# A planner with a new count of instruction blocks and new weights, chunk 3 in a pair, and all decays on VectorE

## The chip, the cores and the metric

The kernel runs on one core of a Trainium2 chip, in float32. Its engines are TensorE (PE, matrix products; PEld is its weight load), VectorE (DVE), ScalarE (ACT), GpSimd (POOL) and SyncE (SP, which here issues DMA transfers). The metric is the device time of one execution in microseconds (us), the median over several runs. The kernel before takes 751.02 us (five runs, 746.96 to 753.35).

## The reference, cut to what matters

A linear attention with a decaying state is computed step by step over 768 tokens, for 4 batches and 8 heads of width 40. Its output goes through a two-layer network with SiLU (320 to 2048 to 320) for all 3072 tokens.

```python
# r, k, v, w, a, b: (4, 8, 768, 40); state: (4, 8, 40, 40)
for t in range(S):
    y[:, :, t] = np.einsum('bhd,bhde->bhe', rt, state)
    Sa = np.einsum('bhde,bhe->bhd', state, at)
    state_decay = state * wt[:, :, None, :] - np.einsum('bhd,bhe->bhde', Sa, bt)
    state = state_decay + np.einsum('bhd,bhe->bhde', vt, kt)
...
x = np.ascontiguousarray(attn_out.transpose(0, 2, 1, 3)).reshape(B * S, H * D)
h = x @ w_in                      # (3072, 320) @ (320, 2048)
g = h * (1.0 / (1.0 + np.exp(-h)))
return (g @ w_out).astype(np.float32)
```

## The kernel before, in words

**Chunks.** The sequence is cut into NN = 12 chunks of 64 tokens. For each chunk the 32 problems (batch and head) are worked at once, and the 256 tokens of the chunk (4 batches of 64) then go through the network. Inside a chunk the step-by-step recurrence is replaced by the inverse of a triangular 64 x 64 matrix for each problem; only the state G passes from chunk to chunk.

**The pieces for chunk n.** `load` and `load_r` read the inputs on SyncE's queue. `prepare` makes running products of the decays with two scans on DVE (L505 and L523, with small helpers L511 to L524 between them), multiplies them onto the inputs (`aside`, L542, writes `kb` for b in two halves and for k in one; `scale`, L532, multiplies `a`), and forms products of tokens with tokens on PE (`between`, L560; `sv`, L621) and transposes (`turn`, L646, copied out by ACT into `kt`). `chain` advances the state: `right` (L987) and its sum into R on DVE (L997), `solve` (L1011), `solve_t` (L1042), the state's transpose (L1072) and `update` (L1099). `read` computes the output: `look` (L1141), `write` (the state's part L1178, the chunk's part L1191) and `scaled` (L1202). `bring` carries it through DRAM into `xt`. `moe` is the network: `full` (L1271), `rest` (L1284), the SiLU `gate` on ACT (L1294), `second` (L1311) and the copy to `ot` (L1323).

**Two ways to the inverse.** Chunks below NS = 4 take `special`: blocks of 16 are inverted on DVE (the multiply L672, the reduction L673 and a copy L696 in `dots` and `steps`), then PE joins them with `both` (L790), `turn` (L803) and three `more` (L835), each followed by an add on DVE (L850). Chunks 4 to 11 are taken two at a time by `inverse(k)`: blocks of 32 of both chunks are inverted on DVE alone, read from `md` in DRAM into `mi` and written back to `zd` and `xd`. Then `merge(n)` brings ZQ and X from there, and joins the blocks with `first` (L915), a copy of ZQ (L283 on ACT, L287 on DVE) and `second` (L944).

**What sets the order.** Nothing is left to the order of the source: every operation is given to the planner `Plan` with its engine, an estimated cost, what it reads and writes, a priority `pri`, the number `k` of its matmuls and the PSUM or SBUF buffers (`Room`) that it needs. `order()` is a list scheduler over all five engines. For each engine it looks at the operations that are ready, and the engine that can start earliest gets one. Among those that can start within SLACK of the earliest it takes the lowest `pri`; when small matmuls have run for more than MOST, it prefers large ones (`k` below 33). `walk` models that PE's instructions are fetched in blocks of 256 and stretches a start where a block would be missing. The list that comes out is written as the program, and each engine runs its own instructions in that order, waiting on semaphores.

**Who computes the decays.** `aside` and `scale` run on DVE for chunks 0 to 3 and on POOL for chunks 4 to 11:

```python
e, cost = ("DVE", 1.25) if n < 4 else ("POOL", 2.6)
add(e, cost + 0.1, partial(aside, e, 1), [vk, bk], ["B"], pri)
add(e, cost, partial(scale, e, A, Z), allw, [("a", i3)], pri)
add(e, cost, partial(aside, e, 0), [vk, kk], ["K"], pri + 0.1)
```

The functions that the change touches:

Of the kernel before, what the change touches and what calls it, by code (L numbers as in the profile page):

```python
# [32 lines left out]
class Plan:  # L33
# [8 lines left out]
    def add(self, engine, cost, do, r=(), w=(), pri=0, rooms=(), k=0, size=0.0, after=0.0):  # L42
        op = dict(
            engine=engine, cost=cost, do=do, pri=pri, rooms=rooms, k=k, size=size, n=len(self.ops), after=after
        )
        before = set()
        for k in r:
            if isinstance(k, tuple) and k[0] == "@":
                before.add(self.wrote[k[1]])
                continue  # L50
            if k in self.wrote:
                before.add(self.wrote[k])
            self.read.setdefault(k, []).append(op["n"])
        for k in w:
            if k in self.wrote:
                before.add(self.wrote[k])
            before.update(self.read.get(k, ()))
            self.wrote[k], self.read[k] = op["n"], []
        before.discard(op["n"])
        op["before"] = before  # L60
        self.ops.append(op)
        return op

    HOP = {"SP": 0.1, "ACT": 0.15, "PE": 0.15, "DVE": 0.15, "POOL": 0.2}
    SLACK = {"SP": 0.0, "ACT": 0.1, "PE": 0.4, "DVE": 0.15, "POOL": 0.1}
    RATE, LAND = 300.0, 2.0
    MOST, SHARE = 1.5, 2.0

    def walk(self, start, cost, k, keep=False):


        fetched, count, t = list(self.fetched), self.count, start
        step = cost / max(k, 1)
        end = count + k
        while True:
            i = len(fetched) - 2
            go, gate = 256 * (i + 1), 256 * (i + 2) - 64
            if count <= go < end:
                t += (go - count) * step
                count = go  # L80
            elif not count > go:
                break
            begin = max(t + 0.4, fetched[-1] + 2.6) if not go < count else max(t, fetched[-1] + 2.6)
            fetched.append(begin + 1.3)
            if gate < end:
                t = max(t + (gate - count) * step, begin + 1.4) if gate > count else max(t, begin + 1.4)
                count = max(count, gate)
        t += (end - count) * step
        if keep:
            self.fetched, self.count = fetched, end  # L90
        return t

    def order(self):
        ops = self.ops
        self.fetched, self.count = [0.0, 0.0], 0
# [7 lines left out]
        mixed, out, held = 0.0, [], {}  # L103
        queue = dict.fromkeys(("SP", "ACT", "POOL"), 0.0)
        for op in ops:
            op["ready"] = op["after"]
        while len(out) < len(ops):
            best = None
            for e, some in ready.items():
                starts = []  # L110
                for op in some:
# [7 lines left out]
                    if e == "PE" and s < 1e8:  # L119
                        lost = self.walk(s, op["cost"], op["k"]) - s - op["cost"]  # L120
# [3 lines left out]
                least = min(x for _, x, _ in starts)  # L124
                near = [x for x in starts if x[1] <= least + self.SLACK[e]]
                if e == "PE" and mixed > self.MOST:
                    near = [x for x in near if x[2]["k"] < 33] or near
                s, _, op = min(near, key=lambda x: (x[2]["pri"], x[2]["n"]))
# [6 lines left out]
            if e == "PE":  # L135
                mixed = mixed + op["cost"] if op["k"] > 32 else max(0.0, mixed - self.SHARE * op["cost"])
            at[e] = end = self.walk(s, op["cost"], op["k"], True) if e == "PE" else s + op["cost"]
# [29 lines left out]
def kernel(  # L167
# [147 lines left out]
    WS, NS, NL, ND, NP = 1024, 4, 0, 1, 3  # L315
# [23 lines left out]
    def weights(n):  # L339
# [42 lines left out]
        for h in range(2):  # L382
            for i in (1, 0):

                def sum_(h=h, i=i):
                    nc.tensor.matmul(
                        pf.tile[:, h],
                        lhsT=ident,
                        rhs=words[:, 512 * h : 512 * h + 512, i].bitcast(F32),
                        start=i == 1,  # L390
                        stop=i == 0,
                    )

                add("PE", 0.97, sum_, me, [(pf, h)], pri, [pf], 2)
# [93 lines left out]
    def prepare(n):  # L488
# [60 lines left out]
        e, cost = ("DVE", 1.25) if n < 4 else ("POOL", 2.6)  # L549
# [19 lines left out]
        add("PE", 1.14, partial(between, 1, pb_), ["B", ("a", i3)], [pb_, ("sb", i2)], pri, [pb_], 128)  # L569
# [17 lines left out]
        else:  # L587
            for b in range(2):
                for c in range(2):
                    q0 = 64 * i2 + 32 * c + 16 * b  # L590
                    r0 = 64 * b + 32 * c
                    dma(
                        lambda q0=q0, r0=r0, c=c: nc.sync.dma_start(
                            md[n // 2 % 2][q0 : q0 + 16].rearrange("q s t -> s q t"),
# [4 lines left out]
                        [("md", n // 2 % 2, i2, b, c)],  # L599
# [3 lines left out]
        add("PE", 1.14, partial(between, 0, pk), ["K", ("a", i3)], [pk], pri + 0.5, [pk, sk], 128)  # L603
# [25 lines left out]
        add("PE", 1.14, sv, [sk, ("v", i2, 0), ("v", i2, 1)], [pv, ("R", i3)], pri + 0.6, [pv, sk], 128)  # L629
# [9 lines left out]
        for b in range(2):  # L639
# [15 lines left out]
            add("PE", 0.75, turn, ["K", "B"], [pt, ("kt", i3, b)], pri + 0.7, [pt], 33)  # L655
# [76 lines left out]
    def special(n):  # L732
# [82 lines left out]
        for part in parts:  # L815
            XI_, X_ = keyed(("XI",), part), keyed(("X2", i2), part)
            k = len(part)
            add("PE", 0.57 * k, partial(both, pm[part], lambda b, g: S_[half(b), g, :], block, part), [("sb", i2), *mik], [pm[part], *XI_], pri, [pm[part]], 64 * k)
            add("PE", 0.3 * k, partial(turn, pd[part], part), mik, [pd[part]], pri, [pd[part]], 16 * k)
# [5 lines left out]
        for k in range(3):  # L825
# [17 lines left out]
            for part in parts:  # L843
                XI_, X_, Y_ = keyed(("XI",), part), keyed(("X2", i2), part), keyed(("tmp",), part)
                l, py = len(part), py_[part]
                add("PE", 0.87 * l, partial(more, part, py), [*XI_, *(Y_ if k else X_)], [py], pri, [py], 64 * l)
# [16 lines left out]
    def inverse(k):  # L863
        i = k % 2
        pri = 10 * (2 * k - 2) + 7
# [15 lines left out]
    def merge(n):  # L881
        pri = 10 * (n - 1) + 5
        i, n2 = n // 2 % 2, n % 2
        X = Xs[n2].rearrange("p (q t) -> p q t", q=Q)
        S_ = sbs[n2].rearrange("p (q t) -> p q t", q=Q)
# [11 lines left out]
        for x in range(2):  # L897
            for c in (1, 0):
# [7 lines left out]
                    [("X", n2, x, c)],  # L906
# [17 lines left out]
        add("PE", 0.8, first, [("sb", n2), ("Zt", 0), ("Zt", 1)], [p1, ("Q", 0), ("Q", 1)], pri, [p1], 128)  # L924
# [28 lines left out]
        add("PE", 1.2, second, [("Q", 0), ("Q", 1), ("X", n2, 0, 1), ("X", n2, 1, 1)], [p2, ("XM", n2, 0), ("XM", n2, 1)], pri, [p2], 128)  # L953
        for x in range(2):
# [8 lines left out]
                [("XM", n2, x)],  # L963
# [4 lines left out]
    def chain(n):  # L968
# [10 lines left out]
        if n:  # L979
# [21 lines left out]
            add("PE", 1.2, right, [("a", i3), "G"], [pa], pri, [pa], 128)  # L1001
            add("DVE", vec(640), total, [pa], [("R", i3)], pri, [pa])
        pw_ = {part: Room("pair", 2) for part in halves(n)}
        if not last:
# [14 lines left out]
            add("PE", 1.14, solve, [*xkeys, ("R", i3)], [pu], pri, [pu], 128)  # L1019
# [39 lines left out]
        for part in halves(n):  # L1059
# [4 lines left out]
            add("PE", 0.57 * l, partial(solve_t, part, pw), [*xp, ("R", i3)], [pw, *[("ut", m) for m in part]], p_, [pw], 64 * l)  # L1064
            add("ACT", act(512 * l), partial(turned, part, pw), [pw], [("ut", m) for m in part], p_, [pw])
        if n:
# [14 lines left out]
            add("PE", 0.75, turn, ["G"], [pt, "GT"], pri + 0.3, [pt], 33)  # L1081
# [11 lines left out]
        if not last:  # L1093
# [13 lines left out]
            add("PE", 1.3, update, [*ktk, *vk, ("u", i2, 0), ("u", i2, 1)], [pg], pri, [pg], 128)  # L1107
# [15 lines left out]
    def read(n):  # L1123
# [8 lines left out]
        for m in range(2):  # L1132
# [16 lines left out]
            add("PE", 1.14, look, rk + vtk + [("ut", m)], [pl], pri, [pl, la], 128)  # L1149
# [15 lines left out]
        py_, yx = {part: Room("pair", 2) for part in parts}, Room("lam", 1)  # L1165
# [6 lines left out]

        def write(part, py):
            if n:
                for o in problems("m", "z", "x", "j", "b"):
                    b, j, x, m, z = (o[k] for k in "bjxmz")
                    hh, c = 8 * j + 4 * m + 2 * z + x, 4 * m + 2 * z + x
                    nc.tensor.matmul(  # L1178
                        py.tile[rows(j), b, c * C : c * C + C],
                        lhsT=GT[rows(b), (8 * j + c) * D : (8 * j + c) * D + D],  # L1180
                        rhs=rs[rows(b), hh, :],
                        start=fresh(py, b, j),
                        stop=False,
                        skip_group_check=True,
                    )
# [23 lines left out]
        for part in parts:  # L1209
            used = [lam[m] for m in part]  # L1210
            cost = 3.05 if n else 0.95 * len(part)
            add("PE", cost, partial(write, part, py_[part]), ktk + rk + used + (["GT"] if n else []), [py_[part]], pri, [py_[part], *used], 256 if n else 64 * len(part))
# [50 lines left out]
    def moe(n):  # L1263
# [4 lines left out]
        def full(g):  # L1268
            for k in range(2):
                for f in range(4):  # L1270
# [4 lines left out]
                        start=g % 2 == 0 and k == 0 and f % 2 == 0,  # L1275
                        stop=g % 2 == 1 and k == 1,
# [3 lines left out]
        def rest(g0):  # L1280
            for g in (g0, g0 + 1):
                for f in (0, 2, 1, 3):
# [5 lines left out]
                        start=g % 2 == 1 and f % 2 == 0,  # L1288
                        stop=g % 2 == 0,
# [9 lines left out]
        for g in (0, 2):  # L1299
            a_, b_ = rooms[g], rooms[g + 1]  # L1300
            w_ = lambda g: [("wi", g)]
            add("PE", 3.6, partial(full, g), [*xk[0], *xk[1], *w_(g)], [a_, ("gts", g), ("gts", g + 1)], pri + g, [a_], 32)
            add("PE", 2.0, partial(rest, g), [*xk[2], *xk[3], ("wi3",)], [a_, b_], pri + g + 0.1, [a_, b_], 32)
            add("PE", 3.6, partial(full, g + 1), [*xk[0], *xk[1], *w_(g + 1)], [b_], pri + g + 0.2, [b_], 32)
# [14 lines left out]
        for b in range(2):  # L1319
            for part in range(4):  # L1320
                need = sorted({("wo", c) for c in range(4 * part * DM // WS, ((4 * part + 4) * DM - 1) // WS + 1)})
                add("PE", 2.17, partial(second, b, part), [("gts", part), ("gts", 3), *need], [po[b]], pri + 4 + b + part * 0.1, [po[b]], 16)
# [23 lines left out]
    for n in range(NN):  # L1346
# [18 lines left out]
        if n + 3 == NS:  # L1365
            eye()
        if n % 2 == 1 and NS < n + 3 < NN + 1:
            inverse(n // 2 + 1)
# [157 lines left out]
```

## Time and profile before

| | before |
|---|---|
| median of five runs | 751.02 us (746.96 to 753.35) |
| profiled execution, its own time | 751.41 us |
| its span | 749.6 us |
| mean granted clock of TensorE | 0.982 |
| PE busy | 683.1 us, 91% |
| DVE busy | 396.0 us, 53% |
| ACT busy | 196.0 us, 26% |
| POOL busy | 81.8 us, 11% |
| longest PE groups | L1311 227.8 us, L1271 178.7 us, L1284 49.0 us |
| decays on POOL | L542 48.4 us in 24 instructions |

The profile is one execution, taken by the hardware profiler. The span is cut into 40 equal slices; a digit is the busy share of an engine in tenths, and `PEclk` is the clock that TensorE was granted, in tenths of full speed. The list of waits says which group of instructions stood idle for whom: total us, number of times, longest. A timeline row gives the start, the time from the first start to the last end, the engine, the source line, what was written and read, the tile, the count, and in brackets the idle time before it with its releaser. A matmul's start to the next one's start is the better measure of its price, since ends are modelled. A matmul in float32 is shown as two instructions, so a call of `second` with four products is eight.

### The profile page before, as it was taken

The numbers are of one execution on the slowest core, as the hardware profiler recorded it, in microseconds if no ns is written. First come the engines' busy times: TensorE is split into PE (matmuls) and PEld (weight loads), VectorE is DVE, ScalarE is ACT, GpSimd is POOL, SyncE is SP. The second block draws the span as 40 slices with busy tenths as digits, with TensorE's granted clock in tenths as the row PEclk, the third lists the DMA queues.
The fourth block names the chain that finished last, engine by engine and source line by source line (L and its number), as shares of the span: only waits on it lengthen the run. The fifth ranks groups of instructions, "written<-read, shape, count | busy, mean of one in ns | idle before, by whom it ended". The sixth has DMA issues, their size and how long they took to land.

```text
span 749.6 us, 27622 instructions
## 1 busy us (share of the span) xinstructions
PE 683.1 (91%) x12810; PEld 540.6 (72%) x12810; DVE 396.0 (53%) x567; ACT 196.0 (26%) x240; POOL 81.8 (11%) x63
## 2 busy tenths in 40 slices
PE   2198898899979998999998999998999999999995
PEld 2176686687768777787777777777777878778773
DVE  6867889574624397245596344496244193320000
ACT  3264355032223113313213113213213203111010
POOL 3200000003004004003220013130013000000000
PEclk9999999999999999899999999999999999999999
DMA  7672833660532434254533344532341403121000
GB/s 245 153 229 74 275 119 94 173 163 17 144 89 87 117 102 88 83 135 126 132 94 73 61 120 130 133 94 66 63 121 44 110 18 84 39 67 40 18 1 22
DMA packets 116956, 75.72 MB, mean 101 GB/s; under 512 B 64546, under 2 KB 113634, under 8 KB 116194
## 3 DMA queue, kind: packets, MB, share of 16 engines
q1 hardware_dynamic: 112328, 63.10, 31.8%
q0 software_dynamic: 2096, 10.49, 4.0%
q8 instruction: 102, 1.67, 0.9%
q10 hardware_dynamic: 2410, 0.30, 0.3%
q14 instruction: 20, 0.16, 0.1%
HBM read 59.64 MB, written 13.83 MB: 98 GB/s over the span
## 4 chain that ended last, share of the span: by engine, by line
PE 62%; DVE 21%; DMA 6%; issue 3%; SPq 3%; ACT 2%; POOL 1%; ACTq 0%; DVEq 0%; POOLq 0%
PE pair L1311 21%; PE pair L1271 14%; DVE XI L672 6%; PE pair L1284 4%; DVE XI L673 4%; DMA wz<-in_wT 3%; PE pair L1141 3%; PE pair L835 3%; PE pair L1191 3%; DVE wz L523 2%; DVE kbv L505 2%; PE pair L560 2%; PE pair L1099 2%; POOL kb L542 1%; PE pair L1178 1%
## 5 line engine op out<-in xcount | busy, mean ns | idle before, releaser
L1311 PE MATMUL pair<-wo,gts 128*128 128x320 f32 x768 | 227.8, 449 | 2.8 <-ACT kt L659 2.8
L1311 PEld LDWEIGHTS pair<-wo,gts 128*128 128x128 f32 x768 | 144.9, 194 | 60.3 <-issue 3.5
L1271 PE MATMUL pair<-xt,wi 128*128 128x256 f32 x768 | 178.7, 387 | 3.9 <-ACT vu L285 1.9
L1271 PEld LDWEIGHTS pair<-xt,wi 128*128 128x128 f32 x768 | 143.8, 192 | 28.6 <-issue 4.0
L1294 ACT ACTIVATE gts<-pair 128x1024 f32<-128x1024 f32 x48 | 49.1, 1023 | 177.5 <-PE pair L1284 88.8
L542 POOL TENSOR_TENSOR kb<-kbv 128x512 f32<-128x512 f32 (+1 forms) x24 | 48.4, 2033 | 324.3 <-DVE wc L512 222.4
L560 PE MATMUL pair<-a,kb 40*64 40x64 f32 x1536 | 30.5, 238 | 28.9 <-DVE a L532 28.9
L560 PEld LDWEIGHTS pair<-a,kb 40*64 40x64 f32 x1536 | 27.8, 151 | 34.1 <-issue 18.4
L1284 PE MATMUL pair<-xt,wi 64*128 64x256 f32 x384 | 49.0, 391 | 3.2 <-DVE ot L1323 2.0
L1323 DVE COPY ot<-pair 128x320 f32<-128x320 f32 x24 | 11.7, 488 | 71.4 <-PE pair L1311 69.7
L673 DVE TENSOR_REDUCE XI<-XI 128x64 f32<-128x512 f32 (+9 forms) x68 | 46.9, 690 | 2.3
L1284 PEld LDWEIGHTS pair<-xt,wi 64*128 64x128 f32 x384 | 35.1, 187 | 12.4 <-issue 5.6
L1153 DVE TENSOR_TENSOR lam<-pair,ml 128x1024 f32<-128x1024 f32 x24 | 29.0, 1220 | 24.1 <-PE pair L1141 24.1
L672 DVE TENSOR_TENSOR XI<-XI,mi 128x1024 f32<-128x1024 f32 (+8 forms) x48 | 36.2, 754 | 5.4 <-DMA mi<-md 4.3
L1202 DVE TENSOR_TENSOR lam<-pair,wz 128x1024 f32<-128x1024 f32 (+1 forms) x13 | 14.8, 1142 | 45.5 <-PE pair L1191 45.3
L523 DVE TENSOR_TENSOR_SCAN wz<-wz,zt 128x1024 f32<-128x1024 f32 x12 | 30.5, 2538 | 0.4
L1141 PEld LDWEIGHTS pair<-r,vut 40*64 40x64 f32 x1536 | 24.8, 135 | 6.1 <-issue 5.3
L606 DVE TENSOR_TENSOR lam<-pair,ml 128x1024 f32<-128x1024 f32 x12 | 14.6, 1220 | 27.2 <-PE pair L560 23.9
L1141 PE MATMUL pair<-r,vut 40*64 40x64 f32 x1536 | 27.7, 221 | 1.1 <-issue 1.0
L505 DVE TENSOR_TENSOR_SCAN kbv<-wz,zt 128x1024 f32<-128x1024 f32 x12 | 27.5, 2292 | 1.0
L1085 ACT COPY GT<-pair 128x640 f32<-128x640 f32 x11 | 7.6, 692 | 74.3 <-PE pair L1072 74.3
L285 ACT ACTIVATE sb<-pair 128x1024 f32<-128x1024 f32 x12 | 12.3, 1022 | 56.3 <-PE pair L560 56.2
(146 smaller groups left out, 728.3 us busy)
## 6 DMA issues: line engine op xcount, KB each, us to landing
wz<-in_wT SPq DMA_DIRECT2D x12, 512.0 KB, 4.2
kbv<-in_bT SPq DMA_DIRECT2D x12, 512.0 KB, 3.6
a<-in_aT SPq DMA_DIRECT2D x12, 512.0 KB, 4.7
kbv<-in_kT SPq DMA_DIRECT2D x12, 512.0 KB, 4.4
r<-in_rT SPq DMA_DIRECT2D x48, 96.0 KB, 2.7
vut<-in_vT SPq DMA_DIRECT2D x48, 96.0 KB, 3.2
vu<-in_v SPq DMA_DIRECT2D x24, 160.0 KB, 4.2
out<-ot SPq DMA_DIRECT2D x48, 80.0 KB, 2.0
```

What stands on the lines that cost most here:

```text
L505: nc.vector.tensor_tensor_scan(back(V), back(W[:, 2 : 2 + Q * C]), zt, 1.0, ALU.mult, ALU.add)
L523: nc.vector.tensor_tensor_scan(Z, Z, zt, 0.0, ALU.mult, ALU.add)
L542: TTn[engine].tensor_tensor(out=at_(kb, place(is_b, first), (576 * step, 4 // step), (128, 4), (1, C)), in0=blocks((kf, bf)[is_b]), in1=bl ...
L560: nc.tensor.matmul(room.tile[half(b), j, g * C : g * C + C], lhsT=kb[rows(j), place(is_b, q) : place(is_b, q) + C], rhs=A[rows(j), q * C : ...
L672: nc.vector.tensor_tensor(out=at_(tmp, 0, *dims), in0=x, in1=y, op=ALU.mult)
L673: nc.vector.tensor_reduce(out=out_, in_=at_(tmp, 0, *dims), axis=AX.X, op=ALU.add)
L1141: nc.tensor.matmul(pl.tile[half(1 - b if role else b), b, c * C : c * C + C], lhsT=vut[rows(b), role, hu, :], rhs=rs[rows(b), hh, :], star ...
L1153: lambda pl=pl, la=la: nc.vector.tensor_tensor(out=la.tile.rearrange("p (q t) -> p q t", q=Q), in0=pl.tile.rearrange("p a b -> p (a b)").r ...
L1271: nc.tensor.matmul(rooms[g].tile[:, f // 2, (f % 2) * T : (f % 2) * T + T], lhsT=wi[:, k, (4 * g + f) * 128 : (4 * g + f) * 128 + 128], rh ...
L1284: nc.tensor.matmul(rooms[g].tile[:, h, (f % 2) * T : (f % 2) * T + T], lhsT=wi3[half(h), g * 256 + (f % 2) * 128 : g * 256 + (f % 2) * 128 ...
L1294: nc.scalar.activation(out=gts[:, 4 * g * T : 4 * g * T + 4 * T], in_=rooms[g].tile.rearrange("p a b -> p (a b)"), func=AF.Silu)
L1311: nc.tensor.matmul(po[b].tile[:, 0, 0:DM], lhsT=g4[:, f, 128 * b : 128 * b + 128], rhs=wo[:, f, :], start=f == 0, stop=f == NF - 1,)
```

## The change

- The planner chooses, on each engine, the operation with the least of (start + time lost + URGE x `pri`) in place of the window SLACK; the limit MOST and SHARE is gone.
- Each PE operation gets a `shape` (F, R, T, Q, H, S); going from one shape to another costs LEAVE of the old and ENTER of the new in the plan.
- `walk` is written anew: blocks are counted as `count // 256`, with a gate at 194 instructions of a block, and a step costs double before 42 us.
- The estimated costs and counts of most PE operations are changed; the estimates don't alter the operations themselves.
- NS goes from 4 to 3: chunks 0 to 2 take `special`; the pairs are (3, 4), (5, 6), (7, 8), (9, 10), and 11 alone. There are five `inverse` and nine `merge` instead of four and eight.
- `aside` and `scale` of every chunk run on DVE.
- `write` is split into two planned operations, `write_state` and `write`.
- `moe` issues full, full, rest for each pair of groups instead of full, rest, full; `second` waits for the last `full` through a key `ff` instead of through the gate buffer.

```diff
-    SLACK = {"SP": 0.0, "ACT": 0.1, "PE": 0.4, "DVE": 0.15, "POOL": 0.1}
     RATE, LAND = 300.0, 2.0
-    MOST, SHARE = 1.5, 2.0
+    COLD = 42.0
+    URGE = {"SP": 0.0, "ACT": 0.03, "PE": 0.05, "DVE": 0.1, "POOL": 0.02}
+    LEAVE = {"F": 0.09, "R": 0.2, "T": 0.13, "Q": 0.13, "H": 0.12, "S": 0.11}
+    ENTER = {"F": 0.08, "R": 0.1, "T": 0.03, "Q": 0.03, "H": 0.03, "S": 0.03}
+
+    def turn(self, op):
+
+        a, b = self.shape, op["shape"]
+        if a == b or {a, b} == {"R", "T"}:
+            return 0.03 if a != "F" else 0.0
+        return self.LEAVE[a] + self.ENTER[b]
...
-        fetched, count, t = list(self.fetched), self.count, start
-        step = cost / max(k, 1)
-        end = count + k
-        while True:
-            i = len(fetched) - 2
-            go, gate = 256 * (i + 1), 256 * (i + 2) - 64
...
+        fetched, count, t = self.fetched[-2:], self.count, start
+        step, end = cost / max(k, 1) * (2 if start < self.COLD else 1), count + k
+        have = len(self.fetched)
+        while count < end:
+            block = count // 256
+            gate = 256 * block + 194
+            if have == block + 1:
+                fetched.append(max(t + 0.4, fetched[-1] + 2.6) + 1.3)
+                have += 1
+            if count >= gate:
+                t = max(t, fetched[-1] + 0.1)
+            to = min(end, gate if count < gate else 256 * block + 256)
+            t += (to - count) * step
+            count = to
...
-                        lost = self.walk(s, op["cost"], op["k"]) - s - op["cost"]
+                        lost = self.walk(s + self.turn(op), op["cost"], op["k"]) - s - op["cost"]
...
-                least = min(x for _, x, _ in starts)
-                near = [x for x in starts if x[1] <= least + self.SLACK[e]]
-                if e == "PE" and mixed > self.MOST:
-                    near = [x for x in near if x[2]["k"] < 33] or near
-                s, _, op = min(near, key=lambda x: (x[2]["pri"], x[2]["n"]))
+                urge = self.URGE[e]
+                s, _, op = min(starts, key=lambda x: (x[1] + urge * x[2]["pri"], x[2]["n"]))
...
-    WS, NS, NL, ND, NP = 1024, 4, 0, 1, 3
+    WS, NS, NL, ND, NP = 1024, 3, 0, 1, 3
...
-        e, cost = ("DVE", 1.25) if n < 4 else ("POOL", 2.6)
+        e, cost = "DVE", 1.25
...
-            cost = 3.05 if n else 0.95 * len(part)
-            add("PE", cost, partial(write, part, py_[part]), ktk + rk + used + (["GT"] if n else []), [py_[part]], pri, [py_[part], *used], 256 if n else 64 * len(part))
+            if n:
+                add("PE", 0.9, partial(write_state, py_[part]), [*rk, "GT"], [py_[part]], pri, [py_[part]], 128)
+            add("PE", 0.87 * len(part), partial(write, part, py_[part]), ktk + used, [py_[part]], pri, [py_[part], *used], 64 * len(part), shape="H")
...
-            add("PE", 3.6, partial(full, g), [*xk[0], *xk[1], *w_(g)], [a_, ("gts", g), ("gts", g + 1)], pri + g, [a_], 32)
-            add("PE", 2.0, partial(rest, g), [*xk[2], *xk[3], ("wi3",)], [a_, b_], pri + g + 0.1, [a_, b_], 32)
-            add("PE", 3.6, partial(full, g + 1), [*xk[0], *xk[1], *w_(g + 1)], [b_], pri + g + 0.2, [b_], 32)
+            for i, x in enumerate((a_, b_)):
+                add("PE", 3.45, partial(full, g + i), [*xk[0], *xk[1], *w_(g + i)], [x, ("ff", n), ("gts", g + i)], pri + g + 0.1 * i, [x], 32, shape="F")
+            add("PE", 1.72, partial(rest, g), [*xk[2], *xk[3], ("wi3",)], [a_, b_], pri + g + 0.2, [a_, b_], 32, shape="R")
...
-        if n + 3 == NS:
-            eye()
-        if n % 2 == 1 and NS < n + 3 < NN + 1:
-            inverse(n // 2 + 1)
+            if n + 3 == NS:
+                eye()
+        if n + 1 >= NS and (n + 1 - NS) % 2 == 0 and n + 1 < NN:
+            inverse((n + 1 - NS) // 2)
```

## The prediction, made before the changed kernel ran

> **What bounds the kernel now.** I read the page first (busy shares, slices, chain), then the waits of TensorE, then the timeline around those waits, and last the granted clock in windows of 3.4 us.
>
> ```profile
> span 749.6 us, 27622 instructions
> PE 683.1 (91%) x12810; PEld 540.6 (72%) x12810; DVE 396.0 (53%) x567; ACT 196.0 (26%) x240; POOL 81.8 (11%) x63
> PE   2198898899979998999998999998999999999995
> DVE  6867889574624397245596344496244193320000
> PEclk9999999999999999899999999999999999999999
> ```
>
> TensorE (PE) is busy for 683 of 749.6 us and close to full in every slice after the third. So what counts is PE's own work, the price of its order, and its few idle places. VectorE (DVE) has 47% free over the whole, but little in slices 5 to 7 (75 to 131 us).
>
> ```profile
> PE pair L560 <- DVE a L532: 28.9, 2, 15.4
> PE pair L790 <- DMA mi<-zs: 3.2, 2, 2.2
> PE pair L835 <- DVE XI L850: 2.7, 2, 2.0
> PE pair L915 <- DMA ZQ<-zd: 2.7, 2, 1.4
> PE pair L646 <- POOL kb L542: 1.9, 1, 1.9
> ```
>
> Columns: total, times, longest. The first row is the start (13.5 and 15.4 us, over at 42 us): it waits for the first chunks' loads and scans, which the change leaves as they are, so it is priced at nothing. All other PE waits together are under 30 us; a new order can win those, what switching between kinds of matmul costs, and the instructions it no longer issues.
>
> ```profile
> 252.28 2.42 PE L1311 MATMUL pair<-wo,gts 128*128 128x320 f32 x8
> 254.63 1.11 PE L1178 MATMUL pair<-r,GT 40*40 40x64 f32 x64
> ...
> 371.72 15.34 PE L1311 MATMUL pair<-wo,gts 128*128 128x320 f32 x56
> 387.00 1.14 PE L987 MATMUL pair<-G,a 40*64 40x40 f32 x64
> ```
>
> Columns: start, time, engine and line. From start to next start, eight L1311 matmuls alone between small ones take 254.63 - 252.28 = 2.35 us; in the long run, (387.00 - 371.72) / 7 = 2.18. So the large side of one interruption is at least 0.17 us, and 0.198 against the 2.153 of the calls inside other runs. On the small side a half of L560 takes 1.09 us between two large ones and 0.93 among small ones: 0.16.
>
> **The change, part by part.** The profiled execution took 751.4 us beside its span of 749.6; the median shown is 751.0, so the sum is made on 751.4 and may stand for the median.
>
> (1) Chunk 3 leaves the special path. PE loses `both` (64 matmuls, 1.09 us), `turn` (0.64) and three `more` (2.01 each): 7.8 us. It gains a `merge` (L915 0.77, L944 1.13): 1.9. Net -5.9. The waits inside that path go too:
>
> ```profile
> 210.73 1.98 PE L790 MATMUL pair<-mi,sb 64*64 64x64 f32 x62 [2.17 <-DMA mi<-zs]
> ...
> 224.37 2.08 PE L835 MATMUL pair<-XI 64*64 64x64 f32 x64 [2.03 <-DVE XI L850]
> ...
> 230.76 2.08 PE L835 MATMUL pair<-XI 64*64 64x64 f32 x64 [0.66 <-DVE XI L850]
> ```
>
> 2.17 + 2.03 + 0.66 = 4.9. After the first, the clock fell:
>
> ```profile
> 206.90:210.30 3.40, 1.65 (x68) 1.12 (x66) 0.49 (x1) 0.69 (x1) 0.00 (x0) 1.00 0.51 113
> 210.30:213.70 3.40, 2.97 (x82) 2.88 (x84) 0.00 (x0) 0.95 (x1) 0.00 (x0) 0.50 0.52 135
> ```
>
> Columns: window, length, busy time of PE, PEld, DVE, ACT, POOL, granted clock. 3.4 us at half clock lose 1.7. Together -5.9 - 4.9 - 1.7 = **-12.5**. Bounds: -14 if the order closes up better, -7.6 if as many us of waits come back around the new merge. There are now five of the 32-step inverses instead of four, and nine merges for eight. The fifth inverse is 31 us of DVE and DMA steps (the four took 31.1, 35.8, 34.9 and 29.5 from the first load to the copy out) in place of the 16-step one of chunk 3; PE's other work hides it, as it hides the four. Without that cover it would be the wait of rival A. On SyncE's queue chunk 3 loses 18 transfers (8 `ms`, `xs`, `zs`, 8 `mi`) and gains 14 (4 `md`, `mi`, 2 `zd`, `xd`, 2 ZQ, 4 X), so what stands behind them there comes no later.
>
> Here a rule of the Trainium skill differs. "TensorE: Matmul & The Clock Gate", section "Why this matters for your kernels", asks for idle gaps of more than about 3 us, one whole window, before the clock halves. The trace halves it after windows with a wait of 2.17 us, and elsewhere after 1.33 us. By the page's rule no 1.7 in this sum would stand.
>
> (2) Fewer interruptions. In the instruction order of the two programs, runs of large matmuls (L1271, L1311, L386) are entered from another line 98 times before and 68 times after. 30 interruptions at between 0.198 (large side alone) and 0.198 + 0.158 = 0.356 us (both sides): -5.9 to -10.7; I take the middle, 30 x 0.277 = **-8.3**.
>
> (3) The planner's count of instruction blocks. PE waits that the profile puts down to "issue" and not to another engine add up to 1.8 (L835) + 1.2 (L1284) + 1.1 (L621) + 1.0 (L1141) = 5.1 us. Whether the new count of 256s is nearer the truth no row shows: 0 to -5.1, I take half, **-2.5**.
>
> (4) Decays from GpSimd (POOL) to DVE, for chunks 4 to 11. DVE gains 16 x 0.688 + 8 x 1.217 (`aside`) + 8 x 1.221 (`scale`) = 30.5 us. It loses what POOL did to it:
>
> ```profile
> 370.50 1.15 DVE L519 COPY wz<-w 128x16 f32<-128x16 f32 x1
> ...
> 371.95 3.11 POOL L542 TENSOR_TENSOR kb<-kbv 128x512 f32<-128x512 f32 x1 [0.34 <-DMA mi<-md]
> ...
> 375.31 2.08 DVE L672 TENSOR_TENSOR XI<-XI,mi 128x16 f32<-128x16 f32 x1
> ```
>
> The copy takes 0.12 us where POOL is idle, and 1.30 on the mean in six places beside POOL (-7.1); the scan L523 2.29 against 3.27 in three (-2.9); three small L672 0.16 to 0.20 against 1.02, 2.08, 2.08 in two inverses (-9.3). So DVE's sum grows by 30.5 - 19.3 = 11.2 us, 1.5% of the span, outside PE's path as a sum. What counts is when. Waits that hang on POOL's decays or on an inverse stretched by them: L646 on `kb` 1.9; L915 on ZQ 1.33 + 1.36; L1284 on `ot` 2.0; L1011 on R 2.5; L1099 2.5: 11.6 us, and four halved windows (two after 299 us, one each at 411.7 and 524.3) 6.8. Of these 18.4 I take half, -9.2, since several also follow from the order.
>
> Against it: in the new order of DVE, after the last step of an inverse, `R` (0.81), `aside` and `scale` (3.8), and at three of the five merges the scan block (3.2) stand ahead of the ZQ copy, for which L944 and the solve wait. Before, DVE idled there:
>
> ```profile
> 404.19 0.81 DVE L997 TENSOR_TENSOR R<-pair,R 128x640 f32<-128x640 f32 x1
> 410.62 0.70 DVE L287 COPY ZQ<-pair 32x512 f32<-32x512 f32 x1 [5.62 <-PE pair L915]
> ```
>
> The room is 410.62 - 404.19 = 6.4 us. 0.81 + 3.8 = 4.6 fits; with the scans 7.8 does not, by 1.4: 3 x 1.4 + 1.7 for one halved window = +5.9. Term: **-3.3**, with bounds -18.4 (all waits gone, all fits) and +15.5 (none gone, 1.4 + 1.7 at each of five merges).
>
> (5) Early stretch, 60 to 180 us, where DVE is at 8 and 9 tenths and the order of `between`, the transposes and the look moves. Before it holds PE waits of 2.8 (L1311 on `kt`, 117 us) and 1.9 (L1271 on `xt`, 145.7 us), each with a halved window of 1.7. If these go: -8; if as many are added: +8. With DVE that full and chunk 4's decays now on it, I take **+4**.
>
> Large, large, rest in `moe` leaves the same matmuls. Both gates of a pair now wait for `rest`, so the second ends one activation (1.02 us) later after PE is done; `second` begins with the earlier parts and the chain's small matmuls are there to fill: nothing. Without that cover it is 12 x 1.02 = 12 us.
>
> Sum: -12.5 - 8.3 - 2.5 - 3.3 + 4 = -22.6; 751.4 - 22.6 = **728.8 us**.
>
> **Rivals.** (A) *No change: PE is quicker and waits.* Terms 1 to 3 give -23.3. If each of five merges finds the inverse late by as much as the longest mid-run wait before (2.8) and pays a halved window (1.7), 5 x 4.5 = 22.5 return: 750.6. For it: two of four L915 already wait on ZQ. Against: those two inverses were the two slowed beside POOL, and the others ended in time.
>
> (B) *Slower: DVE's block ahead of the ZQ copy.* If DVE reaches the merge without slack, 0.81 + 3.8 + 3.2 = 7.8 us stands in full at five merges, each with a halved window: 5 x 9.5 = 47.5, against -23.3 - 9.2: +15.0, 766.4. It decides from 32.5 / 5 = 6.5 us per merge on. For it: the order itself. Against: 5.6 us of idle in that place, and large matmuls of `moe` that PE can run meanwhile.
>
> (C) *The weights don't pay:* an interruption costs its lower bound and "issue" stays: 733.7, still faster.
>
> **How the numbers follow.** My forecast with (C) 0.78; (A) 0.12; (B) 0.10. About 1% (7.5 us) is what a measurement of this kernel can tell from none. Faster by over 1% is 0.78, within it 0.12, slower 0.10. The wide terms are 4 (17 to each side) and 5 (12 and 4); together with the others' 3 each they rarely add up: some 13 down, 715; up to 746, most of the way to (A).
>
> **What would show it.** Right: no POOL decays and L519 at 0.12 throughout; five inverses near 30 us each; PE busy lower by about 14 us; "issue" waits halved; L915, L944, L1011 without waits over 2 us. Wrong: L944 waiting for ZQ by 5 us or more at several merges, halved clocks behind it, or PE idle between 60 and 180 us above 15 us.

## The result, and the profile after

The changed kernel takes 744.81 us (median of 52 runs, 740.96 to 752.37); the kernel before, over all its runs, 749.36. The ratio is 0.9956, with a 95% interval of 0.9942 to 0.9969: 0.4% faster, where 3% was forecast. The profiled execution took 744.37 us, its span is 742.6 against 749.6.

The head of the page after:

```profile
span 742.6 us, 27297 instructions
PE 674.6 (91%) x12666; PEld 543.0 (73%) x12666; DVE 418.6 (56%) x614; ACT 193.8 (26%) x241; POOL 16.4 (2%) x31
PE   2187989898999999999899999999998999999995
DVE  6847679787579346288227595372694576111000
PEclk9999989899999999999799999999998999999998
```

PE is busy 8.5 us less, but its clock digits have more dips. The waits of PE (total, times, longest):

```profile
PE pair L566 <- issue: 16.3, 4, 13.9
PE pair L566 <- DVE a L538: 14.0, 2, 13.4
PE pair L1281 <- DMA xt<-lam: 3.3, 1, 3.3
PE pair L1019 <- issue: 3.0, 2, 1.6
PE pair L1107 <- issue: 2.9, 1, 2.9
PE pair L797 <- issue: 2.8, 1, 2.8
```

The rows on `mi`, XI, ZQ and `kb` that stood here before are gone (the longest such wait left is 0.81 us). In their place is "issue" (13.9 of the first row is the old wait at the start). Two places, from the timeline of PE:

```profile
100.16 1.34 PE L1107 MATMUL pair<-vu,kt 128*40 128x40 f32 x58 [0.65 <-ACT vu L291]
104.40 0.49 PE L1107 MATMUL pair<-vu,kt 128*40 128x40 f32 x6 [2.90 <-issue]
...
390.33 1.14 PE L995 MATMUL pair<-G,a 40*64 40x40 f32 x64
391.29 1.08 PE L1185 MATMUL pair<-r,GT 40*40 40x64 f32 x64
392.51 1.10 PE L1050 MATMUL pair<-X,R 64*40 64x64 f32 x64
393.40 1.01 PE L1019 MATMUL pair<-R,X 64*64 64x40 f32 x52
395.87 0.43 PE L1019 MATMUL pair<-R,X 64*64 64x40 f32 x12 [1.46 <-issue]
```

PE stops in the middle of one operation, which waits for no data. I counted PE's instructions (matmuls, weight loads and the few others) up to each such stop: all 16 of 0.3 us or more after 42 us stand at the same place of a block of 256, three quarters through it. The records of PE's instruction queue (packets, MB, share of the DMA engines) are 16 KB each, 101 of them for PE's 25,444 instructions, so one brings 256:

```profile
q8 instruction: 101, 1.65, 0.9%
```

At each of the 16 stops PE goes on 2.2 to 2.9 us after the last record started, and no two records start less than 3.38 us apart. The timeline lines above show the other side: 128 instructions of `solve_t` last 393.40 - 392.51 = 0.89 us, so small operations use up a block in 1.8 us.

The granted clock around the first of these two places (window, length, busy of PE, PEld, DVE, ACT, POOL, clock, DMA share, GB/s):

```profile
100.10:103.50 3.40, 1.34 (x58) 1.22 (x58) 1.64 (x1) 0.92 (x2) 0.00 (x0) 1.00 1.01 419
103.50:106.90 3.40, 2.50 (x11) 2.07 (x12) 1.83 (x7) 0.00 (x0) 0.00 (x0) 0.50 0.62 255
106.90:110.30 3.40, 3.40 (x9) 2.69 (x9) 3.22 (x4) 0.09 (x1) 0.00 (x0) 0.50 0.00 0
```

**The budget.** Work is PE's busy time less half of the halved windows; waits and windows are counted from 42 us to the last matmul. Each row is one profiled execution.

| kernel | work | issue waits | waits on engines and DMA | lost to the clock | runs of small matmuls of 384 instructions or more after 100 us, longest |
|---|---|---|---|---|---|
| before | 671.2 | 5.0 | 24.6 | 11.9 | 1, 448 |
| changed | 657.6 | 17.7 | 13.2 | 17.0 | 18, 1248 |

Work fell by 13.6 us and waits on engines by 11.4, together 25.0: the size of the forecast gain. Issue waits gave back 12.7 and the clock 5.1. Over all executions timed here the clock's share is larger: span times (1 - granted clock) is 12.2 us on the mean before and 20.3 after, start and end included. The last column counts instructions between two large matmuls. Of the 13 stops after 100 us, ten (9.2 us) lie inside the 18 long runs.

### The profile page after: what moved, and what is told of

It is laid out like the page before. It is cut to its first block, busy times and chain, and to the rows that moved or that the text cites. A ratio compares the mean times of both kernels' runs of the same rounds, so it can differ in the third digit from the quotient of the medians.

```text
span 742.6 us, 27297 instructions
## 1 busy us (share of the span) xinstructions
PE 674.6 (91%) x12666; PEld 543.0 (73%) x12666; DVE 418.6 (56%) x614; ACT 193.8 (26%) x241; POOL 16.4 (2%) x31
## 4 chain that ended last, share of the span: by engine, by line
PE 79%; DVE 8%; issue 5%; DMA 3%; SPq 2%; ACT 2%; ACTq 0%; DVEq 0%
PE pair L1321 27%; PE pair L1281 21%; PE pair L1294 5%; PE pair L1149 3%; PE pair L566 3%; PE pair L1200 3%; PE pair L842 2%; PE pair L1107 2%; PE pair L1019 2%; PE pair L952 2%; PE pair L392 2%; PE pair L628 1%; PE pair L1185 1%; PE pair L1050 1%; PE pair L995 1%
## 5 line engine op out<-in xcount | busy, mean ns | idle before, releaser
L1321 PE MATMUL pair<-wo,gts 128*128 128x320 f32 x768 | 219.9, 443 | 0.9 <-issue 0.9
L1281 PEld LDWEIGHTS pair<-xt,wi 128*128 128x128 f32 x768 | 147.1, 194 | 26.8 <-issue 4.7
L680 DVE TENSOR_REDUCE XI<-XI 128x64 f32<-128x512 f32 (+9 forms) x85 | 58.7, 690 | 2.9
L1161 DVE TENSOR_TENSOR lam<-pair,ml 128x1024 f32<-128x1024 f32 x24 | 29.1, 1222 | 37.7 <-PE pair L1149 37.7
L679 DVE TENSOR_TENSOR XI<-XI,mi 128x1024 f32<-128x1024 f32 (+8 forms) x60 | 33.6, 560 | 2.9 <-DMA mi<-md 1.5
L640 ACT COPY R<-pair 128x640 f32<-128x640 f32 x12 | 8.3, 692 | 98.1 <-PE pair L628 98.1
L548 DVE TENSOR_TENSOR kb<-kbv 128x512 f32<-128x512 f32 (+1 forms) x36 | 30.0, 859 | 0.4
L529 DVE TENSOR_TENSOR_SCAN wz<-wz,zt 128x1024 f32<-128x1024 f32 x12 | 27.5, 2290 | 0.3
L1200 PEld LDWEIGHTS pair<-lam,kt 128*40 128x40 f32 x768 | 22.1, 117 | 5.8 <-issue 3.3
L885 ACT COPY mi<-XI 128x1024 f32<-128x1024 f32 x5 | 10.1, 2017 | 61.8 <-DVE XI L680 61.8
```

Of the source, the lines that this page charges most:

```text
L548: TTn[engine].tensor_tensor(out=at_(kb, place(is_b, first), (576 * step, 4 // step), (128, 4), (1, C)), in0=blocks((kf, bf)[is_b]), in1=bl ...
L679: nc.vector.tensor_tensor(out=at_(tmp, 0, *dims), in0=x, in1=y, op=ALU.mult)
L680: nc.vector.tensor_reduce(out=out_, in_=at_(tmp, 0, *dims), axis=AX.X, op=ALU.add)
L1161: lambda pl=pl, la=la: nc.vector.tensor_tensor(out=la.tile.rearrange("p (q t) -> p q t", q=Q), in0=pl.tile.rearrange("p a b -> p (a b)").r ...
L1200: nc.tensor.matmul(py.tile[rows(j), b, c * C : c * C + C], lhsT=K[:, q, j], rhs=lam[m].tile[:, l * C : l * C + C], start=fresh(py, b, j), ...
L1281: nc.tensor.matmul(rooms[g].tile[:, f // 2, (f % 2) * T : (f % 2) * T + T], lhsT=wi[:, k, (4 * g + f) * 128 : (4 * g + f) * 128 + 128], rh ...
```

## The experiments

Theory F: the gain went into waiting for instruction blocks, which longer runs of small matmuls bring, and into the clock. Theory D: the decays on VectorE take it back. Theory P: the pair does. Each time stands against the kernel before on the same chip. A time is a median of 4 to 12 executions; work, waits and clock are read from the one that was profiled.

**e1, decays on VectorE alone.**

```diff
-        e, cost = ("DVE", 1.25) if n < 4 else ("POOL", 2.6)
+        e, cost = "DVE", 1.25
```

> The kernel before with one part of the change: the decays of all chunks on VectorE, old planner, NS = 4. Theory F (the gain went into TensorE waiting for its instruction blocks, which longer runs of small matmuls bring): this part does not lengthen those runs, so the waits put down to issue stay under 7 us after the start and the POOL waits go; faster by 3 to 12 us. Theory D (the decays on VectorE take the gain back): slower by 5 us or more, with TensorE waits on VectorE. Theory P (the pair costs it): no statement on this run.

740.77 us, ratio 0.9901 (0.9857 to 0.9945). D falls. Issue waits are 6.6 us, waits on engines 17.9 (from 24.6). The copy that took 1.30 us beside GpSimd takes 0.12 in every chunk (minimum, median, maximum in ns):

```profile
L519 DVE COPY wz<-w x12: 121/122/127, 8.5 to 556.9; 128x16 f32<-128x16 f32 x12
```

**e2, the pair alone.**

```diff
-    WS, NS, NL, ND, NP = 1024, 4, 0, 1, 3
+    WS, NS, NL, ND, NP = 1024, 3, 0, 1, 3
```

with the changed indices of `inverse` and `merge`.

> The kernel before with one part of the change: NS = 3, chunk 3 in a pair, old planner, decays on GpSimd from chunk 4. Theory F: the special work of chunk 3 is gone, 8 to 12 us faster, issue waits at most 8 us. Theory P (the fifth inverse comes late and takes the gain back): within 3 us of the kernel before, with TensorE waiting for ZQ, X or the inverse by 5 us or more in new places. Theory D: no statement.

765.28 us, ratio 1.0243 (1.019 to 1.0296): F's expectation was wrong here by 28 us. Work did fall, to 662.9. But PE waits at the merges, as P says, though the loss is more than P's 3 us, and one run of 2592 small instructions appears at 250 us; issue waits are 12.5 us, the clock loses 23.8.

```profile
PE pair L917 <- DMA ZQ<-zd: 7.7, 5, 2.6
PE pair L989 <- issue: 3.2, 1, 3.2
```

**e3, the planner alone** (the changed kernel with NS = 4 and the decays of chunks 4 to 11 on GpSimd).

> The changed kernel with NS = 4 and the decays of chunks 4 to 11 on GpSimd: what is left of the change is the planner (with its new costs, the split of write and the order in moe). Runs of large matmuls are entered 62 times instead of 98. Theory F: 36 x 0.277 = 10 us won on TensorE, and as much or more lost: issue waits of 12 us or more against 5.0, halved clocks behind them; between 5 us faster and 8 us slower than the kernel before. Theories D and P: the planner's own gain is whole here, 10 us or more faster, issue waits at most 7.

770.47 us, ratio 1.0282 (1.0229 to 1.0334). The planner's own part costs 3%: work fell by 6.0 us (10 was forecast for 36 interruptions), issue waits are 12.3, waits on engines 31.9, the clock loses 25.5. F's issue waits came, but its time, at most 8 us slower, didn't: the run is 24 us slower, since waits on engines grew too. D and P, which had the planner's gain whole here, fall.

**e4, the planner without its fetch model.**

```diff
-                t = max(t, fetched[-1] + 0.1)
+                pass
```

> The changed kernel with the planner's line that makes it wait for an instruction block taken out, so that it orders as if blocks were always there. Runs of large matmuls are entered 50 times instead of 68. Theory F: issue waits grow from 17.7 us to 25 or more, and the kernel is 10 to 30 us slower than the changed one. If interruptions are what counts (the price in the prediction): 18 x 0.277 = 5 us faster than the changed one.

785.11 us, ratio 1.047 (1.041 to 1.053), 40 us over the changed kernel. Work is the least of all, 653.0; issue waits are 34.5 us and the clock loses 47.8. Interruptions are not what counts most. Its waits:

```profile
PE pair L566 <- issue: 20.4, 7, 13.9
PE pair L1149 <- issue: 9.2, 9, 1.6
PE pair L1185 <- issue: 3.4, 2, 1.9
```

**e5, pair and decays, old planner** (the diffs of e1 and e2 together).

> The kernel before with two parts of the change, the pair and the decays on VectorE; old planner. The pair alone cost 2.4% and the decays alone won 1%. If the pair's loss came from inverses stretched by GpSimd (waits of L915 on ZQ at every merge), it goes here: 735 us or less, ZQ waits under 1 us in all, and the new planner then costs time in the full change. If it came from the pair itself under the old planner: 755 us or more.

747.05 us, ratio 0.999 (0.9952 to 1.0028), not the 735 or less that was expected. The waits of L917 on ZQ fell from 7.7 to 1.0 us, so GpSimd made most of e2's loss. Of the 15.4 us that the clock still loses, 10.2 stand in one place, a run of 2368 small instructions from 248 us (4.2 us of issue waits in it):

```profile
249.20:252.60 3.40, 1.56 (x114) 1.45 (x104) 1.39 (x2) 1.15 (x2) 0.00 (x0) 1.00 0.59 97
252.60:256.00 3.40, 3.40 (x122) 3.19 (x116) 0.82 (x1) 1.28 (x2) 0.00 (x0) 0.50 0.36 72
262.80:273.00 10.20, 10.20 (x320) 9.87 (x321) 2.86 (x3) 1.39 (x2) 0.00 (x0) 0.50 0.40 114
```

**e6, planner and pair** (the changed kernel with the decays of chunks 4 to 11 on GpSimd), **and e7, planner and decays** (with NS = 4).

> The changed kernel with the decays of chunks 4 to 11 on GpSimd again: planner and pair. If GpSimd's stretching is what makes pair and planner slow alone, this is 15 us or more slower than the changed kernel (760 or more). If the parts simply add up in percent (2.4 + 2.8), 785.

760.25 us, ratio 1.0168 (1.0105 to 1.0231): as forecast, the decays on VectorE are worth some 15 us to the changed kernel.

> The changed kernel with NS = 4: planner and decays on VectorE. Adding the percents of the parts alone: 2.8 - 1.0 = +1.8%, 760 us. If instruction blocks are the planner's main loss, issue waits stay at 11 us or more; if the waits on engines are, issue waits are below 8 us and the time is under 750.

766.14 us, ratio 1.0228 (1.0165 to 1.029); issue waits 16.4 us, clock 28.9. The three parts don't add: alone they give -1.0, +2.4 and +2.8%, all together -0.4%. Each makes another order, and its waits fall anew.

**e8, short loads.**

```diff
-                    dst.rearrange("p (m c) -> p m c", m=B), src[:, n].rearrange("m p c -> p m c")
+                    dst.rearrange("p (m c) -> p m c", m=B)[:, 0:few_], src[0:few_, n].rearrange("m p c -> p m c")
```

with `few_` 1 instead of 4 for b and k from chunk 3 on.

> The changed kernel with the loads of b and k for chunks 3 to 11 cut to a quarter (the rest of these tiles keeps older values, so the output is not the reference's); the order of all instructions is the same. If the fetches of instruction blocks are late because these transfers fill the DMA engines, the issue waits after 160 us (about 11 us) fall to under 5 and the kernel is 6 us or more faster than the changed one. If the pace of fetching itself is the limit, they stay at 8 us or more and the time within 4 us.

742.42 us, ratio 0.9935 (0.9903 to 0.9966), against 0.9956 of the changed kernel. Issue waits after 160 us fell from 10.2 to 5.8 us, between the two expectations. So the transfers are part of why blocks come late, but the time hardly moved: 14.8 us of issue waits remain in all, and the clock lost 20.4.

**e9, e10, e11: the same order, its blocks shifted.** In front of the planned operations:

```diff
+        for _ in range(32):
+            nc.tensor.matmul(pairs[3][0:1, 0, 0:1], lhsT=pad, rhs=pad, start=True, stop=True)
```

8 for e9, 32 for e10, 64 for e11.

> The changed kernel with 8 matmuls of one element put in front of the first of TensorE, while it waits for the loads (32 instructions there). The order of everything else is the same; only the ends of the blocks of 256 instructions move against the work. In the changed kernel every issue wait after the start stands at instruction 193 of a block. Theory F, in the form that the planner's blocks lie wrong against the chip's (it does not count the 104 semaphore instructions that TensorE gets, which bring each gate earlier than planned): moved by 32 the same way, it gets worse, issue waits 18 us or more, 0 to 12 us slower than the changed kernel. If the place of the blocks does not matter: within 2 us of it.

747.12 us, ratio 1.0006 (0.9981 to 1.0031), issue waits 16.8 us.

> The same with 32 such matmuls: 128 instructions, half a block. Theory F in that form: the gates now fall where the planner put long matmuls, issue waits fall from 17.7 to under 8 us, halved windows with them, and the kernel is 8 to 18 us faster than the changed one, 727 to 737 us. If the place of the blocks does not matter: within 2 us of the changed kernel.

747.63 us, ratio 1.0008 (0.9974 to 1.0043), issue waits 18.4 us. That form of F falls: half a block of shift wins nothing.

> The same with 64 such matmuls: 256 instructions, a whole block, so that all later blocks lie as in the changed kernel. Both theories: within 3 us of the changed kernel, issue waits 15 to 20 us. If it is as fast as the shift by 128, the instructions in front help in another way (TensorE's clock or the start).

745.47 us, ratio 0.9976 (0.9949 to 1.0003), issue waits 16.1. In e10 the stops still come three quarters through a block, so at other operations, but several come at nearly the same times, inside the same long runs. Its timeline:

```profile
104.25 0.45 PE L1050 MATMUL pair<-X,R 64*40 64x64 f32 x7 [4.73 <-issue]
...
397.02 0.36 PE L1050 MATMUL pair<-X,R 64*40 64x64 f32 x10 [1.81 <-issue]
```

They were 104.40 in L1107 and 395.87 in L1019. So a stop needs a place three quarters through a block, and what decides most is how much is used up in a stretch: the sum of the stops hardly moves. Where a block ends is not quite without effect: e9 and e10 are half a percent slower than the changed kernel, more than the 2 us allowed for, and no run says why.

**e12, e13: pair and decays, the run at 250 us shortened by the old planner's limit.**

```diff
-    MOST, SHARE = 1.5, 2.0
+    MOST, SHARE = 2.0, 2.0
```

1.2 for e13.

> Pair and decays on VectorE under the old planner, with its limit on small matmuls (MOST) at 2.0 us of planned time instead of 1.5. In the order the run of 2368 small instructions around 260 us is gone; the longest is 544. Theory F: the issue waits (10.6 us) and the halved windows (about 22 us of clock in the mean) of the pair with 1.5 fall to some 6 and 12 us; 730 to 738 us, faster than both kernels. If the pair itself costs (its inverse, its transfers): 742 us or more, as with 1.5.

726.14 us, ratio 0.9711 (0.9669 to 0.9754): the fastest here, faster than both kernels. No run after 100 us is over 416 instructions. In the profiled execution no window between start and end is at half clock; issue waits are 11.3 us, more than the 6 I expected and no less than e5's 10.6, waits on engines 7.4 (e5: 18.1):

```profile
PE 664.3 (92%) x12666; PEld 527.4 (73%) x12666; DVE 418.3 (58%) x614; ACT 197.5 (27%) x241; POOL 13.8 (2%) x31
PEclk9999999999999999999999999999999999999998
```

That execution is the fastest of the six, 720.86 us. Over all six, span times (1 - granted clock) is 7.3 us on the mean, 22.0 in e5, so most of the 21 us between e5 and e12 is clock and none of it issue waits. The limit changes the whole order, so that the long run alone did it is not shown. With this limit the pair itself costs nothing. Work is 664.3 us, more than the changed kernel's 657.6, and the median is 18.7 us lower.

> The same with MOST at 1.2: the longest run is 992, runs of large matmuls are entered 97 times instead of 90. Theory F: between the two, 734 to 742 us, with what is left of issue waits and halved windows at the run of 992. If only the number of interruptions counted: 2 us slower than with 1.5, 749 us.

745.72 us, ratio 0.9968 (0.9936 to 0.9999), not in the 734 to 742 expected. Issue waits fell to 8.4 us, but waits on engines (15.9) and six stretches at half clock (18.7) stay, three of them between 211 and 283 us.

**e14, decays on VectorE and MOST at 2.0, without the pair.**

> The kernel before with the decays on VectorE and MOST at 2.0, without the pair: more runs of 384 and over than with 1.5 (20 against 10 in the order), none over 544. Theory F: 2 to 6 us more of issue waits than with MOST at 1.5 (6.6), a little less work for 4 interruptions fewer; 736 to 744 us, near the 740.8 of MOST 1.5.

738.1 us, ratio 0.9875 (0.9831 to 0.9919), as expected: issue waits 11.3 (e1: 6.6), waits on engines 5.9 (17.9). From e14 to e12 the pair alone is worth 12 us.

**e15, the new planner with a fetch nearer to the traces.**

```diff
-                fetched.append(max(t + 0.4, fetched[-1] + 2.6) + 1.3)
+                fetched.append(max(t + 0.2, fetched[-1] + 1.4) + 2.0)
```

> The changed kernel with the planner's fetch nearer to the traces: a block is there 2.0 us after its fetch begins (1.3 in the changed kernel), fetches may follow each other after 3.4 us (3.9). Runs of large matmuls are entered 82 times instead of 68. Theory F: issue waits fall from 17.7 us to 14 or less and halved windows with them, work grows by 14 x 0.277 = 4 us; 736 to 746 us. If fetching is not the cause: 4 us slower than the changed kernel, 749.

740.34 us, ratio 0.9895 (0.9862 to 0.9929), clear of the changed kernel's interval. Issue waits are 10.1 us, work grew by 3.5 (4 expected), six runs of 384 or more are left instead of 18. In the profile the halved windows did not fall (17.1 us, 17.0 in the changed kernel), and waits on engines rose from 13.2 to 17.3; over all its executions the clock's share is 15.9 us on the mean against 20.3.

**e16, the new planner with a term against long runs.**

```diff
+                late = lambda x: 1.0 if e == "PE" and x[2]["k"] > 32 and small + x[2]["k"] > 256 else 0.0
-                s, _, op = min(starts, key=lambda x: (x[1] + urge * x[2]["pri"], x[2]["n"]))
+                s, _, op = min(starts, key=lambda x: (x[1] + urge * x[2]["pri"] + late(x), x[2]["n"]))
```

> The changed kernel with one term more in the planner's choice: an operation of small matmuls that would bring the unbroken run of them over 256 instructions counts as 1 us later. Runs of large matmuls are entered 89 times instead of 68. Theory F: issue waits fall from 17.7 us to under 12, halved windows from 20 us of clock in the mean to under 15, work grows by 21 x 0.277 = 6 us; 732 to 742 us, faster than the changed kernel. If it is the new planner's other parts that cost: 748 us or more, for the 6 us of work.

745.14 us, ratio 0.9954 (0.9925 to 0.9983). Issue waits fell as F says, from 17.7 to 6.4 us, and two runs are left. The time didn't: PE waited for other things, 27.0 us in all, 7.8 of them once for the chain's output on its way into `xt`.

```profile
PE pair L1283 <- DMA xt<-xh: 8.2, 2, 7.8
PE pair L1283 <- DVE wi L386: 5.7, 1, 5.7
```

**e17, e12 with the decays on GpSimd.**

> The kernel before with the pair and MOST at 2.0, decays of chunks 4 to 11 on GpSimd: e12 without the decays on VectorE. If GpSimd's part in the inverses costs what it did under MOST at 1.5 (765 against 747 us): 740 to 746 us, with TensorE waits of L917 on ZQ of 5 us and halved windows behind them. If the long run alone made that difference: within 4 us of 726.

747.94 us, ratio 0.9998 (0.997 to 1.0026), 22 us over e12. That is more than the 740 to 746 expected. No run is over 416, but waits on engines are 20.0 us (3.3 of them L917 on ZQ, 5 were expected) and the clock loses 17.0. So long runs are one way to lose the clock, and the decays on GpSimd, with the waits that they bring, another.

## Why the prediction was right or wrong

| step | forecast | measured |
|---|---|---|
| 1 and 2, PE's work (5.9 + 8.3) | -14.2 | -13.6 |
| waits on engines and DMA (4.9 of step 1, 5.8 - 4.2 of step 4) | -6.5, and step 5's part of +4 | -11.4 |
| 3, issue | -2.5 | **+12.7** |
| halved windows (steps 1 and 4) | -3.4 | **+5.1** |

**Steps 1 and 2** came out in the sum, in part by luck: alone, the pair took 8.3 us off the work (e2), the planner 6.0 for 36 interruptions (e3) and the decays 2.4 (e1). Per interruption e3, e4, e15 and e16 give 0.12 to 0.26 us of work, less than my 0.277.

**Step 3 failed.** I took "issue" as a rest of which half would go, with a bound of 0 above. It was the counterpart of step 2. Before, the longest run of small matmuls after 100 us had 448 instructions; 30 fewer entries made 18 runs of 384 and more, and those outrun the fetch. e4 pushes that on (34.5 us of issue, 40 us slower, less work) and e15 and e16 draw it back (10.1 and 6.4). Over the runs, issue waits go with the number of such runs: 5.0 to 8.4 us with one to three, 10.1 to 13.0 with six to ten, 12.3 to 18.4 with 17 to 19 and 34.5 with e4's 16; e2 and e5, each with a run of over 2300, have 12.5 and 10.6. Fewer issue waits alone are not a faster kernel, as e16 shows. Nothing in my working priced what a longer run needs, though the timeline of before held one number (128 small instructions in under a us) and the instruction queue's records the other.

**The clock, steps 1 and 4.** I counted one halved window (1.7 us) for a wait, and expected fewer. But the clock often stays low for two or three windows: the changed kernel has four stretches at half clock of 6.8, 6.8, 10.2 and 6.8 us, and one of 3.4.

**Step 4** had the right sign and was too small: alone the decays win 1%, 7.4 us of 746.7, against my 3.3; with the pair they are worth 18 us (e2 to e5), in the changed kernel 15 (e6) and in e12 22 (e17). The wait that I feared, VectorE's block ahead of the ZQ copy, is not there: no wait of L952 for ZQ is over 0.4 us. Rival B falls with it, and D with e1.

**Step 5** was near by luck: PE is busy for 106.5 us of the 120 from 60 to 180 us, 110.7 before, so 4.2 us more is idle. But that is not VectorE being full (which it is at 8 and 9 tenths only from 75 to 131 us): waits on engines and DMA fell there from 8.1 to 7.7 us, and issue waits rose from 1.2 to 5.7. On top of that come the halved windows, five instead of two: as much as the whole 5.1 us in the table.

**Rivals.** The outcome is nearest to A, less 1% but not its mechanism: no merge waits 2.8 us for the inverse. That three parts of the change together give 0.4% while two of them with a limit of 2.0 give 2.9% was in no rival. Of the signs that I named, no decays on GpSimd, the short copy (now L525) at 0.12 us and merges without waits over 2 us came; PE's busy time fell by 8.5 us instead of 14, and issue waits, which were to halve, grew more than threefold.

**Fetching, against a page.** The Trainium skill, "Runtime: NRT & Kernel Launch", section "Instruction fetch mechanics", has blocks of 256 instructions of 16 KB, which these records show, and says that fetching is hidden because instructions are dispatched more slowly than they are filled in. On PE the runs differ: 34.5 us of it stood open in e4.

**What stays open.** Which order gets all of it is not settled. MOST at 1.2, 1.5 and 2.0 gives 746, 747 and 726 us; a small change of the planner moves the time by 20 us, and I can name the waits afterwards, not ahead. Apart from the count of blocks (e4, e15), which part of the new planner (weights, costs, order in `moe`) makes the long runs was not tried. In the profiles e12's 18.7 us of waits halve the clock nowhere, where e1's 24.5 do six times. Part of that is this one execution: it lost about 3 us to the clock, start and end included, the slowest of e12's six about 12. Why the others lose more with the same order, no run takes apart.

## What to carry to other kernels

A long run of small matmuls has a price that no single row shows: it can use instructions faster than they are fetched, and each stop in it may halve the clock. Before a planner is told to switch less, find from the trace how many instructions lie between two large operations and what a block of instructions costs to bring. And when several parts of a change each make a new order, don't judge a part alone: here the pair costs 2.4% by itself and is worth 12 us in the fastest version.

## What the runs showed of the hardware that I had not expected

**The clock's windows.** All halved stretches of an execution start on one grid of 3.41 us. In eight of the profiles (before, changed, e1, e2, e4, e5, e7, e10), cut on that grid, the clock halved after 65 windows. Of the 34 windows at full clock in which PE was busy for less than 52%, 32 were followed by one at half clock; the other two are in the kernel before, at 43 and 221 us. Between 52 and 86% 33 of 149 were, and 32 of these hold mostly small matmuls, as do 82 of the 116 that were not. Above 86% none was.

**A short stop is enough.** The Trainium skill ("TensorE: Matmul & The Clock Gate", section "Why this matters for your kernels") lets the clock drop after one idle window. Here it dropped after windows in which PE was busy for more than half, as at 356 us of the changed kernel, where the stops are 0.34 and 1.27 us, the second still open when the window ends:

```profile
354.79 0.56 PE L952 MATMUL pair<-X,ZQ 32*32 32x32 f32 x23 [0.34 <-DVE ZQ L293]
356.62 1.28 PE L952 MATMUL pair<-X,ZQ 32*32 32x32 f32 x41 [1.27 <-issue]
...
352.70:356.10 3.40, 2.31 (x151) 2.03 (x152) 0.70 (x1) 2.00 (x4) 0.00 (x0) 1.00 0.75 120
356.10:359.50 3.40, 2.88 (x103) 2.81 (x105) 0.69 (x1) 0.57 (x1) 0.00 (x0) 0.50 0.91 196
```

A stop as long does not always do it: the 1.46 us before 395.87 us were followed by full clock.

**The fetch and other transfers.** The longest stop of the changed kernel and that of e10 stand where the loads of the weights `w_out` fill the DMA engines: 2.90 us at 104 us, with a DMA share of 1.01 in the window above, and 4.73 in e10. That these loads delay the fetch is not shown; e8 shows it for the loads of b and k, in part.
